# Four reorderings in a two-layer attention and MLP kernel: early split of the output weights, query features tile by tile, norm transposes behind output products, keys woven by fifths

## The chip, the cores and the metric

The kernel runs on one core of a Trainium2 chip. The metric is the time of one execution on the device in microseconds (us), the median of several runs. The engines are TensorE (PE, matrix products, with its weight loads counted apart as PEld), VectorE (DVE), ScalarE (ACT), GpSimd (POOL) and SyncE (SP), which issues nearly all of the DMA transfers. Each engine works through its own list of instructions in order and waits on semaphores for the others.

## The reference

Two equal layers follow each other on x of 2048 rows (S) by 576 columns (D), in f32. In each layer:

```
n = layernorm(x);  q, k, v = n @ wqkv                    # 32 heads of 18 columns
pq = q @ w_phi (per head);  pk = k @ w_phi
phi_q = [softmax(pq), softmax(-pq)];  phi_k likewise     # 36 features a head
kv = phi_k^T v;   z = sum of phi_k over the rows
x = x + ((phi_q kv) / (phi_q z + 1e-6)) @ wo
h = relu(layernorm(x) @ w1 + b1)^2                       # 4608 hidden columns
x = x + h @ w2 + b2
```

Keys of all rows are needed before the first query of a layer can be finished, since kv and z sum over all rows.

## The kernel before

**Tiles and precision.** The rows stand in four blocks of 512, each of four row tiles of 128. Every f32 operand of a large product is split in a high and a low part (names ending in h and l: ACT copies the high part, DVE or POOL subtracts it to leave the low one), and a product is three matrix products: high by high, low by high, high by low.

**Order of the work.** At the start the feature matrix w_phi is folded into the query and key weights (`g_fold`), which is woven with the norm of block 0. Then come the first keys: for three blocks `g_keys` projects v and k by row tile (v0, k0), makes the key features (K: DVE maxima, POOL and ACT for the exponentials, DVE sums, POOL scaling) and adds a tile to kv (kvp, two tiles later), woven with the next block's norm (n0). The last block's keys end in `barrier`, where z and the scaled kv matrices (ko, kt, kbh, kbl) are made, the queries' features of one block are finished (`g_phi`, names t0f in layer 0 and t1f in layer 1: products fm, sums fu, factors, scaled features fQ0e to fQ3e, one for each row tile), and `g_out` makes its attention output: transposes of the features (opt), products with kv (opn, split in ooh, ool and the last piece oolt), output products (opo) with the output weights (oo), added to x (ox). Its norm (onm, onn, one) and that norm's transposes (onp) follow in the same function. Then come the MLP of two blocks one by one (m with the block's number), and of the other two blocks as a pair (names m_p), whose second half is `seconds`: for each of 36 hidden tiles 12 products by rows (pach, pacacc0 to pacacc2) and 3 for the remaining features (pacacc3). In layer 0 that half is woven with `back_keys`, which norms a finished block for layer 1 (n1_3, n1_2, n1_0), projects its v and k and adds them to kv.

**The norm's transposes.** A norm makes four row tiles (n0 to n3). Each is transposed in four pieces on PE into a PSUM tile (p0 to p3), and the columns left over of two row tiles go into one further tile (p40, p41). ACT copies the high part out, DVE subtracts the low one (L413), and only then is the tile of PSUM free. The bank used by p40 is released by the subtraction for p0.

**What sets the order.** Generators are woven by hand: `weave(main, other, rate)` gives the second generator `rate` units of cost at every step of the first. A scheduler then places the instructions of each engine by priority in program order, and may take one ahead of another where its operands are ready by its own estimate. `tc.issue_after` keeps an instruction behind a given one; `held` does that for named instructions, and `chained` (L129) keeps everything that a step of a generator issues on DVE, ACT and POOL behind the last instruction that its earlier steps issued there, but leaves PE and SP free.

**Output weights.** In layer 0 `g_out` loads the raw output weights in the barrier (`wpiece`, L320 and L322), splits them there (ACT copies, and POOL subtracts, L331) and stores the parts in DRAM (wsoh, wsol, L352) for later loads; in layer 1 it loads the stored parts.

Of the kernel before, what the change touches and what calls it, by code (L numbers as in the profile page):

```python
# [21 lines left out]
def layers_kernel(  # L22
# [210 lines left out]
    def g_fold(kpair, vpair):  # L233
# [41 lines left out]
        def times(k, wt):  # L275
# [39 lines left out]
    def wpiece(src, c0, name, tags=TAGS_A, heads=False, low=None):  # L315
        raw = sb.tile([P, NC, HP], F32, tag="wraw", name=f"{name}r", bufs=2)
        hi, lo = piece_tiles(name, tags)
        if heads:
            full = (NG - 1) * GW
            nc.sync.dma_start(raw[:GW, : NG - 1],  # L320
                              src[:full, c0 : c0 + HP].rearrange("(g p) n -> p g n", p=GW))
            nc.sync.dma_start(raw[: gw[-1], NG - 1], src[full:, c0 : c0 + HP])  # L322
            parts = [(slice(0, GW), slice(0, NG - 1)), (slice(0, gw[-1]), slice(NG - 1, NG))]
        else:
            nc.sync.dma_start(raw[:, :KC],
                              src[: KC * P, c0 : c0 + HP].rearrange("(c p) n -> p c n", p=P))
            load_twice(raw[:, KC], src, c0, HP)
            parts = [(slice(0, P), slice(0, NC))]
        for p, c in parts:
            nc.scalar.activation(hi[p, c], raw[p, c], AF.Copy)  # L330
            (low or nc.vector).tensor_sub(lo[p, c], raw[p, c], hi[p, c].bitcast(F32))  # L331
        return hi, lo

    def wpair(which, name, tags=TAGS_A, low=None):
        if which in kept and tags is TAGS_A:
            return [wloaded(which, h, f"{name}{which}{h}", tags) for h in range(2)]
        if which == "o":
            return [wpiece(wo, h * HP, f"{name}o{h}", tags, heads=True, low=low) for h in range(2)]
        return [wpiece(wf, (which == "k") * D + h * HP, f"{name}{which}{h}", tags) for h in range(2)]

# [40 lines left out]
    def g_norm(x_of, dst, name, then=None, fine=False):  # L381
# [57 lines left out]

        if not fine:  # L440
# [302 lines left out]
    def g_out(layer, b, ph, dst, name, parts=1, pause=None, behind=None, norm=None, mid=None, costs=(None, None)):  # L743
# [46 lines left out]
        def pieces():  # L790
            with tc.issue_after(behind.ins) if behind else nullcontext():
                return wpair("o", name, low=nc.gpsimd if parts > 1 else None)

        def x_after(t):
# [3 lines left out]
            for half in range(2):  # L798
                hi, lo = pair[half]
                pt = wtile(f"{name}po{half}{t}")  # L800
                for g in range(NG):
                    w = gw[g]
                    l = ol[:w, g, rows] if g < KC else olt[:w, rows]
                    for k, (a, m) in enumerate(((oh[:w, g, rows], hi), (oh[:w, g, rows], lo), (l, hi))):
                        nc.tensor.matmul(pt[:, :HP], a, m[:w, g], start=(g == 0 and k == 0),  # L805
                                         stop=(g == NG - 1 and k == 2))
                cols = slice(half * HP, (half + 1) * HP)
                nc.vector.tensor_add(x[:, cols], pt[:, :HP], x[:, cols])
            return x

        pair = pieces() if behind or "o" in kept else None
        if pair:
            keep_split("o", pair)
# [11 lines left out]
        pair = pair or pieces()  # L825

# [4 lines left out]
        def x_next(t):  # L831
            return xs_of[t] if t < len(xs_of) else x_after(t)
# [12 lines left out]

    def g_mlp(layer, b, x, after, name, rest=None, then=None):
# [82 lines left out]
        if rest:  # L929
            with tc.issue_after(dense["hidden"].ins):  # L930
                drain(rest)
# [649 lines left out]
```

## Time and profile before

| | us |
|---|---|
| median of 3 runs | 2532.76 |
| lowest, highest | 2530.81, 2532.87 |
| the profiled execution | 2538.57 |
| its span in the profile | 2536.8 |
| PE busy in it | 2481.7 |
| DVE, ACT, POOL busy | 1570.9, 1265.5, 949.5 |

The profiled execution is 5.8 us above the median, and 1.8 us of it lie outside the span. The mean granted clock of PE is 0.992 of the full one. In the rows of the profile a name such as n_2p stands for all buffers of that name (p0 to p41 of the norm of block 2), "<-" separates what is written from what is read, and a bracket at the end tells how long the engine idled before the row and which instruction released it. L numbers are lines of the kernel before; the changed kernel's lines are some 7 to 24 higher.

### The profile page before, as it was taken

The page shows a single profiled execution, that of the slowest core. Times are in us where ns is not written, and L with a number is a line of the kernel's source. Part 1 is how long each engine was busy: PE and PEld are TensorE (multiplying, and loading weights), DVE is VectorE, ACT ScalarE, POOL GpSimd, SP SyncE. Part 2 cuts the span into 40 slices and gives each one's busy share as a digit, 9 for nine tenths or more (in the row PEclk, how much of TensorE's full clock was granted, in tenths as well). Part 3 has the DMA queues.
Part 4 walks back from the last instruction along what each step waited for, and adds up shares of the span by engine and source line. Part 5 has one row for each costly group of instructions (what it writes and reads, how often), then busy time and mean ns, then how long its engine had stood idle before and what let it go on. Part 6 is the DMA issues. An engine that isn't in the chain of part 4 may idle for free.

```text
span 2536.8 us, 41468 instructions
## 1 busy us (share of the span) xinstructions
PE 2481.7 (98%) x15108; PEld 2179.8 (86%) x15108; DVE 1570.9 (62%) x2514; ACT 1265.5 (50%) x2245; POOL 949.5 (37%) x1101
## 2 busy tenths in 40 slices
PE   8998999999999999999999989999999999999999
PEld 8997888889888888888889988888898888888888
DVE  6778848554856655554667679394548566555444
ACT  4344545443446666663333435454445466666642
POOL 3544312212325555551333333031123355565322
PEclk8999999999999999999999999999999999999999
DMA  9222643356434433328654134333563444333363
GB/s 326 79 69 91 196 116 85 103 164 213 133 119 125 143 114 99 113 93 295 206 180 148 47 128 150 102 99 98 166 222 112 129 130 142 116 96 109 112 199 127
DMA packets 249691, 348.52 MB, mean 137 GB/s; under 512 B 30158, under 2 KB 157262, under 8 KB 246926
## 3 DMA queue, kind: packets, MB, share of 16 engines
q1 hardware_dynamic: 248228, 343.18, 42.7%
q8 instruction: 118, 1.93, 0.3%
q10 hardware_dynamic: 1258, 2.70, 0.3%
q14 instruction: 87, 0.71, 0.1%
HBM read 279.46 MB, written 66.32 MB: 136 GB/s over the span
## 4 chain that ended last, share of the span: by engine, by line
PE 47%; DVE 3%; DMA 2%; ACT 1%; POOL 1%; issue 1%; SPq 0%; DVEq 0%; ACTq 0%; POOLq 0%
PE m_1ph L887 5%; PE m_0ph L887 4%; PE m_pacacc L1231 4%; PE m_ppx L1202 4%; PE m_1acc L914 3%; PE m_0acc L914 3%; PE m_pacc L1231 3%; PE m_ppy L1202 2%; PE m_pacacc L1221 2%; PE m_pach L1231 1%; PE m_0acc L905 1%; PE m_1acc L905 1%; PE m_pacc L1221 1%; PE m_ppz L1202 1%; PE a_0po L805 1%
## 5 line engine op out<-in xcount | busy, mean ns | idle before, releaser
L1192 POOL TENSOR_TENSOR m_ps<-m_pr,m_ps 128x128 fp32r<-128x128 f32 x144 | 118.2, 821 | 338.6 <-ACT m_ps L1190 282.9
L1191 DVE TENSOR_TENSOR m_ps<-m_pr,m_ps 128x448 fp32r<-128x448 f32 x144 | 98.1, 681 | 194.7 <-ACT m_ps L1190 191.3
L1231 PE MATMUL m_pacc<-m_ps,m_phb 128*128 128x448 f32 x864 | 188.5, 366 | 0.0
L1231 PEld LDWEIGHTS m_pacc<-m_ps,m_phb 128*128 128x128 f32 x864 | 162.2, 188 | 18.0
L1190 ACT ACTIVATE m_ps<-m_pr 128x576 fp32r<-128x576 f32 x144 | 98.1, 681 | 154.5 <-issue 88.2
L1231 PE MATMUL m_pacacc<-m_ps,m_phc 128*128 128x448 f32 x648 | 147.7, 370 | 0.0
L1231 PEld LDWEIGHTS m_pacacc<-m_ps,m_phc 128*128 128x128 f32 x648 | 122.6, 190 | 9.9
L1212 DVE TENSOR_TENSOR m_phb<-m_pz,m_phb 128x512 fp32r<-128x512 f32 x72 | 56.5, 784 | 113.1 <-ACT m_pz L1211 111.6
L914 PE MATMUL m_2acc<-m_2s,m_2hb 128*128 128x448 f32 x432 | 100.2, 366 | 0.0
L914 PE MATMUL m_0acc<-m_0s,m_0hb 128*128 128x448 f32 x432 | 100.1, 366 | 0.0
L887 PE MATMUL m_3ph<-t0onh,m_3h 128*128 128x512 f32 (+1 forms) x380 | 98.0, 383 | 1.6 <-DVE t0onh L426 0.8
L914 PE MATMUL m_1acc<-m_1s,m_1hb 128*128 128x448 f32 x432 | 99.4, 365 | 0.0
L914 PE MATMUL m_3acc<-m_3s,m_3hb 128*128 128x448 f32 x432 | 99.4, 365 | 0.0
L887 PE MATMUL m_1ph<-t1onh,m_1h 128*128 128x512 f32 (+1 forms) x380 | 97.8, 382 | 1.5 <-DVE t1onh L426 0.8
L887 PE MATMUL m_0ph<-a_0nh,m_0h 128*128 128x512 f32 (+1 forms) x380 | 97.8, 384 | 0.0
L887 PE MATMUL m_2ph<-a_2nh,m_2h 128*128 128x512 f32 (+1 forms) x380 | 97.8, 384 | 0.0
L914 PEld LDWEIGHTS m_2acc<-m_2s,m_2hb 128*128 128x128 f32 x432 | 80.9, 188 | 10.5 <-ACT m_2hb L895 0.2
L914 PEld LDWEIGHTS m_0acc<-m_0s,m_0hb 128*128 128x128 f32 x432 | 80.9, 188 | 10.6 <-ACT m_0hb L895 0.2
L914 PEld LDWEIGHTS m_1acc<-m_1s,m_1hb 128*128 128x128 f32 x432 | 81.1, 188 | 10.3
L914 PEld LDWEIGHTS m_3acc<-m_3s,m_3hb 128*128 128x128 f32 x432 | 81.1, 188 | 10.3
L872 POOL TENSOR_TENSOR m_3s<-m_3r,m_3s 128x128 fp32r<-128x128 f32 x36 | 24.6, 683 | 168.6 <-ACT m_3s L867 154.1
L872 POOL TENSOR_TENSOR m_1s<-m_1r,m_1s 128x128 fp32r<-128x128 f32 x36 | 24.7, 686 | 167.7 <-ACT m_1s L867 153.3
(2440 smaller groups left out, 7372.1 us busy)
## 6 DMA issues: line engine op xcount, KB each, us to landing
m_pr<-in_B_w SPq DMA_DIRECT2D x144, 288.0 KB
m_pr<-in_B_w SPq DMA_DIRECT2D x72, 256.0 KB
hd<-m_pu SPq DMA_DIRECT2D x72, 256.0 KB
m_pg<-hd SPq DMA_DIRECT2D x72, 256.0 KB
m_3r<-in_B_w SPq DMA_DIRECT2D x36, 288.0 KB
m_2r<-in_B_w SPq DMA_DIRECT2D x36, 288.0 KB
m_1r<-in_B_w SPq DMA_DIRECT2D x36, 288.0 KB
m_0r<-in_B_w SPq DMA_DIRECT2D x36, 288.0 KB
```

Source lines behind the costliest of these rows:

```text
L805: nc.tensor.matmul(pt[:, :HP], a, m[:w, g], start=(g == 0 and k == 0), stop=(g == NG - 1 and k == 2))
L872: nc.gpsimd.tensor_sub(s2[:, D + R : 2 * D], r2[:, R:], s2[:, R:D].bitcast(F32))
L887: dense["hidden"] = nc.tensor.matmul(ph[:, cols], a, m, start=(k == 0), stop=(k == len(ops) - 1))
L905: nc.tensor.matmul(acc[KC], a, m, start=(f == 0 and k == 0), stop=(f == NF - 1 and k == 2))
L914: nc.tensor.matmul(acc[t][:, :R], a[:, rows], m, start=(f == 0 and k == 0), stop=(f == NF - 1 and k == 2))
L1190: nc.scalar.activation(s2[:, :D], r2, AF.Copy)
L1191: nc.vector.tensor_sub(s2[:, D : D + R], r2[:, :R], s2[:, :R].bitcast(F32))
L1192: nc.gpsimd.tensor_sub(s2[:, D + R : 2 * D], r2[:, R:], s2[:, R:D].bitcast(F32))
L1202: nc.tensor.matmul(ps, a, m, start=start and i == 0, stop=i == len(ms) - 1, skip_group_check=True)
L1212: nc.vector.tensor_sub(hl, r, hh.bitcast(F32))
L1221: nc.tensor.matmul(accs[b][KC], a, m, start=(g == 0 and k == 0), stop=(g == NF - 1 and k == 2))
L1231: nc.tensor.matmul(accs[b][t][:, :R], a[:, rows], m, start=(g == 0 and k == 0), stop=(g == NF - 1 and k == 2))
```

## The change

**V's split in the fold.** In `g_fold` the split of the v weights runs one chunk behind.

**Output weights.** A new generator `g_split` loads the raw output weights in five groups (wsr0 to wsr4, four of 126 rows and one of 72), splits each (wss: high part on ACT, low part on DVE) and stores both parts in DRAM. `g_keys` advances it by one step at each row tile of the first keys. The barrier of layer 0 now loads the split parts as layer 1 does; the loads, copies, POOL subtractions and stores that it had are gone. The raw groups use the buffers named r2, which the first hidden tiles' weights use too, and the split groups use the two places of kbh and kbl.

**Query features.** In `barrier` the generator `g_phi` is wrapped in `chained`.

**Norm in the barrier.** `g_out` with two parts no longer draws the norm step by step between the output products: it scales two row tiles, makes the output products, and issues the transposes of a row tile behind a named last output product. The last tile's part is a function that the MLP calls.

**Keys' side.** `seconds` yields five times for a hidden tile (after the products of each row tile and after the remaining features) in place of once, the rate of the weave goes from 4.0 to 0.8, and `chained` gets a strict form that also keeps PE's instructions of `back_keys` behind those that stand ahead of them in the program.

```diff
-    def chained(gen):
+    def chained(gen, strict=False):
...
             mark = len(traced)
+            if strict:
+                ends[nc.tensor.engine] = next(i for i in reversed(traced) if i.engine == nc.tensor.engine)
             with ExitStack() as behind:
...
+            for c in ([c - 1] if i == 2 and c else []) + ([c] if i == 2 and c == KC else []):
                 for half in range(2):
                     hi, lo = (piece[:, c] for piece in vpair[half])
...
+    def g_split():
+
+        for g in range(NG):
+            w = gw[g]
+            raw = sb.tile([P, D], F32, tag="r2", name=f"wsr{g}")
+            nc.sync.dma_start(raw[:w], wo[g * GW : g * GW + w])
+            both = cst.tile([P, 2 * NG * GW], F32R, tag=("kbh", "kbl")[g % 2], name=f"wss{g}")
+            hi, lo = both[:w, :D], both[:w, D : 2 * D]
+            nc.scalar.activation(hi, raw[:w], AF.Copy)
+            yield
+            nc.vector.tensor_sub(lo, raw[:w], hi.bitcast(F32))
+            for part, home in zip((hi, lo), wsplit["o"]):
+                nc.sync.dma_start(home[:w].rearrange("p (h c n) -> p h c n", h=2, c=NC)[:, :, g],
+                                  part.rearrange("p (h n) -> p h n", h=2).bitcast(F32))
+            yield
...
-        pair = pieces() if behind or "o" in kept else None
-        if pair:
-            keep_split("o", pair)
+        pair = wpair("o", name)
...
-        norms = (norm or g_norm)(x_next, dst, f"{name}n", keep)
-        for t in range(len(xs_of)):
-            for _ in held(norms, ("part",)):
-                break
-        if xs_of:
-            for _ in range(NT - len(xs_of)):
-                next(norms)
-            dense["rest"] = norms
+        if not xs_of:
+            yield from paced((norm or g_norm)(x_after, dst, f"{name}n", keep), costs[1])
             return
-        yield from paced(norms, costs[1])
+        scale, turn_rows, turn_rest = next(g_norm(xs_of.__getitem__, dst, f"{name}n", keep, None))
+
+        def behind_out(call, *args):
+            with tc.issue_after(dense["out"].ins):
+                call(*args)
+
+        with tc.issue_after(dense["part"].ins):
+            xns = [scale(t) for t in range(2)]
+        xs_of.append(x_after(2))
+        behind_out(turn_rows, 0, xns[0])
+        other = g_after(3)
+        next(other)
+        behind_out(turn_rows, 1, xns[1])
+        behind_out(turn_rest, 0)
+        xs_of.append(next(other))
+        xns.append(scale(2))
+        behind_out(turn_rows, 2, xns[2])
+        xns.append(scale(3))
...
-                second(f)
+                for t in range(NT):
+                    by_rows(f, [t], range(3))
+                    yield
+                features(f, range(3))
+                del high[f], wide[f]
                 yield
...
-        phi = g_phi(layer, er, ph, f"{n}f")
+        phi = chained(g_phi(layer, er, ph, f"{n}f"))
...
+    splits = g_split()
...
             yield
+            next(splits, None)
             e = soft_k(raw, f"K0_{b}_{t}")
...
-        back = iter(()) if layer else chained(back_keys())
+        back = iter(()) if layer else chained(back_keys(), True)
...
-        weave(seconds, back, 4.0)
+        weave(seconds, back, 0.8)
```

The first place is SP's list in the first keys, before and after (x0_2 is the input of block 2, xth and xtl are spills of a norm, t0q0r raw query weights):

```order
L467 DMA xtl0_105<-n0_0l_385 128x2048
L1357 DMA x0_2_0_1148<-in_A_x 128x576
L1357 DMA x0_2_1_1226<-in_A_x 128x576
L1357 DMA x0_2_2_1356<-in_A_x 128x576
L1357 DMA x0_2_3_1424<-in_A_x 128x576
L325 DMA t0q0r_2333<-wf_109 128x4x288
L227 DMA t0q0r_2333<-wf_109 64x288 x2
L325 DMA t0q1r_2341<-wf_109 128x4x288
```

```order
L337 DMA wsr2_1118<-in_A_wo 126x576
L1381 DMA x0_2_0_1166<-in_A_x 128x576
L1381 DMA x0_2_1_1244<-in_A_x 128x576
L1381 DMA x0_2_2_1377<-in_A_x 128x576
L344 DMA wsoh_116<-wss2_1120 252x1x288
L337 DMA wsr3_1402<-in_A_wo 126x576
L1381 DMA x0_2_3_1449<-in_A_x 128x576
L1381 DMA x0_3_0_1707<-in_A_x 128x576
L321 DMA t0q0r_2368<-wf_109 128x4x288
L344 DMA wsol_117<-wss2_1120 252x1x288
L344 DMA wsoh_116<-wss3_1404 252x1x288
L337 DMA wsr4_1659<-in_A_wo 72x576
```

The load of wsr3 and the last of x0_2 now stand behind a store of wss2, and the load of wsr4 behind a store of wss3; both stores wait for subtractions on DVE.

The second place is POOL's list in the barrier of layer 0, before and after (oo0l and oo1l are low parts of the output weights, fm the products and fQe the scaled features of the queries):

```order
L331 TENSOR_TENSOR t0oo0l_2992<-t0oo0r_2990,t0oo0h_2991 126x1152
L331 TENSOR_TENSOR t0oo0l_2992<-t0oo0r_2990,t0oo0h_2991 72x288
L331 TENSOR_TENSOR t0oo1l_3001<-t0oo1r_2999,t0oo1h_3000 126x1152
L694 TENSOR_TENSOR t0fm01_2836<-t0fQ0e_2549,zb0_2802 128x576
L331 TENSOR_TENSOR t0oo1l_3001<-t0oo1r_2999,t0oo1h_3000 72x288
L694 TENSOR_TENSOR t0fm11_2913<-t0fQ1e_2556,zb0_2802 128x576
L712 TENSOR_TENSOR t0fQ0e_2549<-t0fQ0e_2549,t0fQ0r_2626 128x576
L694 TENSOR_TENSOR t0fm21_2981<-t0fQ2e_2630,zb0_2802 128x576
L712 TENSOR_TENSOR t0fQ1e_2556<-t0fQ1e_2556,t0fQ1r_2700 128x576
```

```order
L704 TENSOR_TENSOR t0fm01_2871<-t0fQ0e_2584,zb0_2837 128x576
L722 TENSOR_TENSOR t0fQ0e_2584<-t0fQ0e_2584,t0fQ0r_2661 128x576
L704 TENSOR_TENSOR t0fm11_2948<-t0fQ1e_2591,zb0_2837 128x576
L722 TENSOR_TENSOR t0fQ1e_2591<-t0fQ1e_2591,t0fQ1r_2735 128x576
L892 TENSOR_TENSOR m0_3s2_0_3503<-m0_3r2_0_3497,m0_3s2_0_3503 128x128
L704 TENSOR_TENSOR t0fm21_3016<-t0fQ2e_2665,zb0_2837 128x576
```

The four subtractions of the output weights are gone, and the product for the second row tile (fm11) stands behind the scaling of the first (fQ0e).

The third place is PE's list where the norm of block 2 for layer 1 meets the hidden tiles 48 and 49 of the pair, before and after:

```order
L1231 MATMUL m0_pacacc1_11997<-m0_ps2_48_12687,m0_phc48_12693 128x448 x3
L1231 MATMUL m0_pacacc2_11998<-m0_ps2_48_12687,m0_phc48_12693 128x448 x3
L1221 MATMUL m0_pacacc3_11999<-m0_phc48_12693,m0_ps2_48_12687 128x512 x3
L404 MATMUL n1_2p0_12911<-ident_157,n1_2n0_12817 128x128 x4
L404 MATMUL n1_2p1_12920<-ident_157,n1_2n1_12830 128x128 x4
L1231 MATMUL m0_pach_11995<-m0_ps2_49_12750,m0_phc49_12756 128x448 x3
L1231 MATMUL m0_pacacc0_11996<-m0_ps2_49_12750,m0_phc49_12756 128x448 x3
L418 MATMUL n1_2p40_12927<-ident_157,n1_2e_12806 128x128 x2
L1231 MATMUL m0_pacacc1_11997<-m0_ps2_49_12750,m0_phc49_12756 128x448 x3
L1231 MATMUL m0_pacacc2_11998<-m0_ps2_49_12750,m0_phc49_12756 128x448 x3
L1221 MATMUL m0_pacacc3_11999<-m0_phc49_12756,m0_ps2_49_12750 128x512 x3
L404 MATMUL n1_2p2_12958<-ident_157,n1_2n2_12869 128x128 x4
```

```order
L1251 MATMUL m0_pacacc1_12018<-m0_ps2_48_12708,m0_phc48_12714 128x448 x3
L411 MATMUL n1_2p0_12926<-ident_157,n1_2n0_12829 128x128 x4
L1251 MATMUL m0_pacacc2_12019<-m0_ps2_48_12708,m0_phc48_12714 128x448 x3
L411 MATMUL n1_2p1_12938<-ident_157,n1_2n1_12851 128x128 x4
L1241 MATMUL m0_pacacc3_12020<-m0_phc48_12714,m0_ps2_48_12708 128x512 x3
L425 MATMUL n1_2p40_12948<-ident_157,n1_2e_12818 128x128 x2
L1251 MATMUL m0_pach_12016<-m0_ps2_49_12771,m0_phc49_12777 128x448 x3
L411 MATMUL n1_2p2_12967<-ident_157,n1_2n2_12881 128x128 x4
L1251 MATMUL m0_pacacc0_12017<-m0_ps2_49_12771,m0_phc49_12777 128x448 x3
L1251 MATMUL m0_pacacc1_12018<-m0_ps2_49_12771,m0_phc49_12777 128x448 x3
L411 MATMUL n1_2p3_12977<-ident_157,n1_2n3_12903 128x128 x4
L1251 MATMUL m0_pacacc2_12019<-m0_ps2_49_12771,m0_phc49_12777 128x448 x3
```

The transposes now stand between the products of single row tiles, and those of the remainder (n1_2p40) stand ahead of the six products pach and pacacc0 of hidden tile 49, behind which they stood.

More of the change, by code (lines that the diff above doesn't have):

```diff
@@ L741, in g_features, with g_out @@
                                  (2.6, 0.4, 3.0, 2.8, 1.2)), ("last", "squared"))
-    def g_out(layer, b, ph, dst, name, parts=1, pause=None, behind=None, norm=None, mid=None, costs=(None, None)):
+    def g_out(layer, b, ph, dst, name, parts=1, pause=None, norm=None, mid=None, costs=(None, None)):
         kbh, kbl = sums[layer]["kb"]
@@ L788, in times, with g_after @@
                 dense["part"] = nc.vector.tensor_sub(lo, pn[:w, :pw], oh[:w, g, cols].bitcast(F32))
[L790 to L794, printed above, removed]
+        def g_after(t):
             x = sb.tile([P, D], F32, tag="x", name=f"{name}x{t}", bufs=5)
@@ L1371, in g_attend @@
             yield from mid[0]
-        yield from g_out(layer, b, ph, dst, name, behind=behind and behind["last"], norm=norm, mid=mid[1],
+        yield from g_out(layer, b, ph, dst, name, norm=norm, mid=mid[1],
                          costs=(1.0, None if norm else 3.0))
```

48 lines of the change are left out of this document (21 added, 27 removed).

## Prediction

> **What bounds the kernel now.** I read the page's busy times first, then the table of waits for TensorE (PE), then a table of stages with the granted clock, and last single stretches of the engines in order of time.
>
> ```profile
> PE 2481.7 (98%) x15108; PEld 2179.8 (86%) x15108; DVE 1570.9 (62%) x2514; ACT 1265.5 (50%) x2245; POOL 949.5 (37%) x1101
> ```
> ```profile
> PE n_2p L418 <- DVE n_2l L413: 6.1, 1, 6.1
> PE n_0p L418 <- DVE n_0l L413: 5.6, 1, 5.6
> PE t0opt L768 <- DVE t0fQ1e L712: 3.5, 1, 3.5
> ...
> PE t1onp L404 <- DVE t1onn L393: 2.3, 3, 1.3
> PE t0onp L404 <- DVE t0onn L393: 2.3, 3, 1.3
> PE kt L631 <- DVE kq L625: 2.2, 1, 2.2
> PE t1opt L768 <- DVE t1fQ1e L712: 2.0, 1, 2.0
> PE k_3kp L484 <- DMA w_3k0h<-wskh: 1.9, 1, 1.9
> PE n_3p L418 <- DVE n_3l L413: 1.8, 1, 1.8
> ...
> PE t0opt L768 <- DVE t0fQ0e L712: 1.2, 1, 1.2
> ```
> ```profile
> 30.00:180.00 150.00, 148.12 (x1800) 144.92 (x1801) 112.76 (x181) 57.54 (x114) 66.60 (x58) 0.98 0.41 145
> 180.00:260.00 80.00, 68.60 (x742) 65.58 (x742) 67.41 (x122) 30.68 (x67) 40.33 (x33) 0.96 0.29 96
> ...
> 1180.00:1386.00 206.00, 192.43 (x1595) 177.21 (x1594) 127.56 (x177) 72.91 (x125) 71.90 (x69) 0.96 0.57 195
> ...
> 1470.00:1520.00 50.00, 43.25 (x322) 41.03 (x322) 38.24 (x88) 18.74 (x47) 20.29 (x21) 0.97 0.40 138
> ```
> PE is busy 98% of the time, and the number of matrix products stays the same, so only two things can move: its idle time (2536.8 − 2481.7 = 55 us of span) and a lowered clock. In the table of stages the columns are PE, PEld, DVE, ACT, POOL, then PE's granted clock. The idle time lies where the change works: the barrier of layer 0 (180 to 260: 11.4 us), the keys woven behind the last hidden tiles (1180 to 1386: 13.6 us) and the barrier of layer 1 (1470 to 1520: 6.8 us). These stretches also have the low clocks: 0.96 over 206 us is up to 8.2 us of speed, less what of it falls on idle time. One such place, groups of the same product before and after the 6.1 us wait:
>
> ```profile
> 1238.91 1.96 PE L1231 MATMUL m_pacacc<-m_ps,m_phc 128*128 128x448 f32 x9
> ...
> 1252.91 0.69 PE L418 MATMUL n_2p<-ident,n_2e 128*128 128x128 f32 x2 [6.13 <-DVE n_2l L413]
> 1253.25 2.59 PE L1231 MATMUL m_pacacc<-m_ps,m_phc 128*128 128x448 f32 x6
> ```
> One product takes 1.96 / 9 = 0.22 us before and 2.59 / 6 = 0.43 us after: a wait costs its length and then some 2 us of halved clock. In layer 1 a wait of only 2.0 us is followed by the same (0.97 over 50 us is 1.5 us).
>
> **Output weights split early.** In the barrier of layer 0, POOL subtracts four pieces of the output weights; layer 1, which loads split weights, has no such work and is the model of after. Product z begins both stretches, the last low part (oolt) ends them:
>
> ```profile
> 195.96 2.01 PE L589 MATMUL z<-kv,top 128*128 128x126 f32 x16
> ...
> 228.00 0.42 DVE L788 TENSOR_TENSOR t0oolt<-t0opn,t0ooh 72x256 fp32r<-72x256 f32 x1 [0.82 <-ACT t0ooh L786]
> ```
> ```profile
> 1456.64 1.99 PE L589 MATMUL z<-kv,top 128*128 128x126 f32 x16
> ...
> 1482.97 0.42 DVE L788 TENSOR_TENSOR t1oolt<-t1opn,t1ooh 72x256 fp32r<-72x256 f32 x1 [0.83 <-ACT t1ooh L786]
> ```
> 32.0 us against 26.3 us: **−5.7 us**. The cause shows on VectorE (DVE) and POOL:
>
> ```profile
> 198.04 3.94 POOL L331 TENSOR_TENSOR t0oo0l<-t0oo0r,t0oo0h 126x1152 fp32r<-126x1152 f32 x2 [4.82 <-ACT t0oo0h L330]
> ...
> 201.38 7.77 DVE L605 TENSOR_TENSOR kbl<-ko,kbh 126x504 fp32r<-126x504 f32 x2
> ...
> 1462.01 2.37 DVE L605 TENSOR_TENSOR kbl<-ko,kbh 126x504 fp32r<-126x504 f32 x2
> ```
> The same two subtractions take 7.77 us beside POOL's and 2.37 us without, 5.4 us of the 5.7. [...]
>
> The new place is the first keys: five loads, five ACT copies, five DVE subtractions and ten stores, all in a stage where PE is busy 148.12 of 150 us. What covers them is the slack of the keys:
>
> ```profile
> 68.64 0.41 ACT L502 ACTIVATE k_0s<-k_0p 128x288 f32<-128x288 f32 x1 [0.62 <-PE k_0p L484]
> ...
> 74.69 1.17 ACT L528 ACTIVATE K_3e<-K_3e 128x1152 f32<-128x1152 f32 x1 [2.05 <-DVE n_1h L426]
> ```
> ```profile
> 78.30 2.15 POOL L544 TENSOR_TENSOR K_3e<-K_3e,K_3r 128x1152 f32<-128x1152 f32 x1 [3.64 <-DVE K_3r L533]
> ...
> 88.79 2.15 POOL L544 TENSOR_TENSOR K_0e<-K_0e,K_0r 128x1152 f32<-128x1152 f32 x1 [3.55 <-ACT n_2h L412]
> ```
> ```profile
> 87.98 0.77 PE L573 MATMUL kvp<-K_3e,vslot 128*32 128x36 f32 x64
> ...
> 96.93 0.77 PE L573 MATMUL kvp<-K_0e,vslot 128*32 128x36 f32 x64
> ```
> ```profile
> DMA  8999920576747009999896910000000000810000
> ```
> ```profile
> 47.34 11.52 SPq L1357 DMA_DIRECT2D x<-in_A_x  x4
> ```
> ```profile
> 61.31 0.75 DVE L375 BATCH_NORM_STATS2 n_2s<-x 128x6 f32<-128x288 f32 x2
> ```
> PE uses K_3 at 87.98, ready at 80.45, and the next K_0 at 96.93, ready at 90.94: 7.5 and 6.0 us of slack. SP works in order. There wsr3 is now loaded behind the store of wss2, which waits for DVE at about 72, and so is the last x of block 2. How long a landing takes lies between some 1.1 us (288 KB at 274 GB/s, the rate before 30 us) and 14.0 us (the x issued at 47.34, used at 61.31, with the DMA full). The DMA's busy tenths above run from 60 us in slices of 1 us: from 65 on it has gaps and stands at 0 at 73 and 74, so I estimate 2.5 to 3: wsr3 lands at 75.3, while ACT stands before its copy from 68 on, with k_0s behind it. K_3 then comes 5 us late (cover left: 2.5). wsr4 in turn stands behind the store of wss3 (about 86) and lands at 89; ACT waits for it with the evictions behind it. PE has seven tiles of PSUM to run ahead, 1.9 us each; the eighth is wanted at 88.7 and free at 89.7, and K_0 is 1 us late as well: **+2 us** (0 with the quick landing, +18 with the slow one). The V split that lags a chunk, on ACT before 40 us, I cost at nothing, since the same copies and subtractions are issued, some a chunk later; bounds ±1 by estimate.
>
> **Query features by tile.** On DVE the product fm20 and its sum no longer stand ahead of fQ1e, for which PE waits:
>
> ```profile
> 1470.59 1.73 DVE L694 TENSOR_TENSOR t1fm<-t1fQ2e,zb 128x576 f32<-128x576 f32 x1
> ...
> 1472.38 0.74 DVE L700 TENSOR_REDUCE t1fu<-t1fm 128x32 f32<-128x576 f32 x1
> 1473.04 1.34 DVE L712 TENSOR_TENSOR t1fQ1e<-t1fQ1e,t1fQ1r 128x576 f32<-128x576 f32 x1
> ```
> ```profile
> 1461.29 1.95 POOL L694 TENSOR_TENSOR t1fm<-t1fQ1e,zb 128x576 f32<-128x576 f32 x1
> ```
> That takes 2.47 us out; but POOL's fm11, done at 1463.2 before, now stands behind POOL's half of fQ0e, and DVE must wait for it. Counting the chain through, fQ1e comes 1.6 us earlier. I take **−1.5 us in each layer, −3.0**, near the wait it shortens. Ends: +0.8 (the serial fm11 is the longer chain) and −3.7 (the wait of 2.0 and its 1.5 to 1.7 us of clock go whole).
>
> **Norm's transposes behind output products.** In each layer three waits of 2.3 us together (onp). The transposes move behind 5 to 12 more output products, about to the point where the rows are scaled. **−2.0 in each layer, −4.0.** Ends: 0 (the DVE chain of the norm is the bound and the wait returns at the next hidden product) and −4.6.
>
> **Keys' side by fifths.** Three norms stall PE by 1.8 + 6.1 + 5.6 us. PE wants the remainder's transposes (p40), whose PSUM bank comes free with DVE's n_l, late in this chain:
>
> ```profile
> 1249.40 0.67 DVE L393 TENSOR_SCALAR n_2n<-x,n_2m,n_2d 128x512 f32<-128x512 f32 x1 [0.98 <-POOL n_2d L378]
> ...
> 1252.16 1.29 DVE L413 TENSOR_TENSOR n_2l<-n_2p,n_2h 128x512 fp32r<-128x512 f32 x2
> ```
> After the change p40 stands 8, 6 and 9 to 12 products of 0.22 us earlier on PE in the three norms: 1.8, 1.3 and 2.0 to 2.6 us more to wait. DVE's chain comes earlier too, since the projections ahead do: 0.6, about 2 and 0 to 2 us. So n_3p 3.0, n_2p 5.4, n_0p 6 or so: 14.4 against 13.5. **+1.0 us**, nothing taken for the next key weights (k_2kp), whose load gets less time before its use; it may come to wait as k_3kp's does, 1.9 us. Ends: −15.7 (the waits of n_2p and n_0p go, with 4 us of clock) and +11.
>
> [...]
>
> **The sum.** The profiled execution took 2538.57 us, 1.8 us of it outside the span, and lies 5.8 us above the median of 2532.76. −5.7 + 2 − 3 − 4 + 1 = −9.7 us: 2528.9 by the profiled execution, **2523** by the median.
>
> **Rivals.**
> - The fifths do feed PE: DVE catches up behind smaller pieces, and the two long waits go with their clock. For it speaks that PE's supply is finer; against it that p40 stands earlier. −15.7 in place of +1: 2506.
> - The first keys stall (slower): wsr3 lands after 14 us as the x did, at 86.6. ACT's evictions stop, PE runs out of PSUM tiles near 82 (5 us), K_3 misses its slack by 4, wsr4 costs 3, and two halved stretches 6: +18 in place of +2, 2539. Against it: the DMA is no longer full at 72. It decides from a landing past 84 or so.
> - The stalls of the fifths grow to the upper end, +11 in place of +1 (n_0p 2.6, n_3p and its clock 2.9, n_2p 2, key weights 1.9 with 1.6 of clock): 2533, no change.
> - The two reorderings in the barriers don't do what they say, as the norm's and the features' chains on DVE are as long as before: 0 in place of −7, 2530.
>
> **Chances.** Forecast 0.48 (its own range 2517 to 2530), fifths feed 0.10, first keys stall 0.15, fifths' stalls grow 0.15, reorderings empty 0.12. About 0.2%, 5 us, is what a measurement of this kernel can tell from no change: 2527.7 to 2537.8. Faster: 0.43 + 0.10 + 0.03 = 0.56; slower: 0.11 from the first keys and 0.04 from the fifths = 0.15; the rest, 0.29, is the same. The range leaves out most of the fifths' gain and the worst of the first keys: 2512 to 2540.
>
> **What would show it.** Right: kbl<-ko,kbh near 2.4 us in both layers; the waits for kq and t0fQ0e gone, for fQ1e under 1 us; no onp wait over 0.5 us; n_2p and n_0p still waiting 4 us or more; no PE wait over 2 us between 60 and 110. Wrong: evictions on ACT behind wss3 or wss4 with PE idle there; or the n_p waits gone, or longer than 7 us.

## The result, and the profile after

| | before | after |
|---|---|---|
| median of the runs shown | 2532.52 us (4 runs) | 2553.24 us (4 runs, 2551.80 to 2554.89) |
| ratio to before, 95% interval | 1 | 1.0083 [1.0066, 1.0101] |
| profiled execution | 2538.57 us, span 2536.8, clock 0.992 | 2554.89 us, span 2553.2, clock 0.990 |

The change makes the kernel 20.7 us slower. The forecast was 2523 us, and its range ended at 2540.

The page of the changed kernel, busy times; as many products as before, 7.8 us more of them (part of them at half clock), and 8.6 us more idle time of PE (2553.2 − 2489.5 against 2536.8 − 2481.7):

```profile
PE 2489.5 (98%) x15108; PEld 2186.2 (86%) x15108; DVE 1567.1 (61%) x2519; ACT 1265.0 (50%) x2246; POOL 944.3 (37%) x1097
```

The table of PE's waits of the changed kernel (who was waited for, us in total, times, longest):

```profile
PE n_0p L425 <- DVE n_0l L420: 4.7, 1, 4.7
PE n_2p L425 <- DVE n_2l L420: 4.6, 1, 4.6
...
PE kvp L583 <- issue: 3.6, 1, 3.6
PE t0opt L778 <- DVE kbl L615: 3.0, 1, 3.0
PE t1opt L778 <- DVE kbl L615: 3.0, 1, 3.0
PE t1opt L778 <- DVE t1fQ3e L722: 2.9, 1, 2.9
PE t0opt L778 <- DVE t0fQ3e L722: 2.9, 1, 2.9
...
PE a_3qp L494 <- issue: 2.1, 1, 2.1
...
PE n_3p L425 <- DVE n_3l L420: 1.5, 2, 1.1
PE t1onp L411 <- DVE t1onn L400: 1.4, 3, 0.7
PE t0onp L411 <- DVE t0onn L400: 1.3, 2, 0.7
```

The waits that the change aimed at are shorter: fQ1e is gone from the top, the onp waits fell from 2.3 us a layer to 1.4 and 1.3, the three norms of the woven keys wait 10.8 us in place of 13.5. Six others stand in their place: kbl and fQ3e in both layers (11.8 us, against 0.9 for each fQ3e before, shown below), and two waits for "issue", in the kvp products of layer 0 and at the first product of a_3q in layer 1. Before the change:

```profile
PE t1opt L768 <- DVE t1fQ3e L712: 0.9, 1, 0.9
```

The changed kernel's table of the stages that the prediction showed (stretch, PE, PEld, DVE, ACT, POOL, PE's granted clock, DMA share, GB/s):

```profile
30.00:180.00 150.00, 146.85 (x1788) 143.30 (x1788) 118.53 (x181) 56.19 (x115) 67.36 (x57) 0.98 0.46 159
180.00:260.00 80.00, 67.93 (x712) 65.31 (x711) 59.27 (x115) 27.64 (x64) 30.83 (x25) 0.91 0.22 69
1180.00:1386.00 206.00, 195.88 (x1625) 180.35 (x1626) 125.05 (x181) 76.25 (x132) 71.81 (x71) 0.98 0.60 206
1470.00:1520.00 50.00, 41.72 (x288) 39.72 (x287) 36.49 (x81) 16.66 (x43) 20.82 (x19) 0.90 0.20 62
```

The loss lies in the two barriers. Their clock fell from 0.96 to 0.91 and from 0.97 to 0.90, and in the first of them PE passes 712 products in the 80 us shown where it passed 742 (its work there starts 1.1 us later). The woven keys (third row) are better than before, with clock 0.98 against 0.96.

Matching PE's products of the two profiles by name gives the offset of after to before from place to place: +2.2 us in the first keys, +7.0 in the barrier of layer 0, −6.4 in the woven keys, +11.4 in the barrier of layer 1, and +2.2 in the rest, together the 16.4 us by which the span grew.

**Where VectorE stops.** DVE of the changed kernel in the barrier of layer 1, from fQ1e to the two last low parts of the attention output (oolt):

```profile
1476.14 0.76 DVE L722 TENSOR_TENSOR t1fQ1e<-t1fQ1e,t1fQ1r 128x576 f32<-128x576 f32 x1
1476.82 1.72 DVE L704 TENSOR_TENSOR t1fm<-t1fQ2e,zb 128x576 f32<-128x576 f32 x1
1480.24 1.41 DVE L710 TENSOR_REDUCE t1fu<-t1fm 128x32 f32<-128x576 f32 x2 [1.70 <-POOL t1fm L704]
1481.57 0.29 DVE L615 TENSOR_TENSOR kbl<-kt,kbh 72x144 fp32r<-72x144 f32 x1
...
1490.56 0.42 DVE L798 TENSOR_TENSOR t1oolt<-t1opn,t1ooh 72x256 fp32r<-72x256 f32 x1 [0.82 <-ACT t1ooh L796]
...
1508.98 0.42 DVE L798 TENSOR_TENSOR t1oolt<-t1opn,t1ooh 72x256 fp32r<-72x256 f32 x1 [0.59 <-ACT t1ooh L796]
```

The same stretch of POOL:

```profile
1476.25 1.67 POOL L722 TENSOR_TENSOR t1fQ1e<-t1fQ1e,t1fQ1r 128x576 f32<-128x576 f32 x1 [2.72 <-DVE t1fQ1r L717]
1477.89 0.97 POOL L892 TENSOR_TENSOR m_1s<-m_1r,m_1s 128x128 fp32r<-128x128 f32 x1
1478.82 1.39 POOL L704 TENSOR_TENSOR t1fm<-t1fQ2e,zb 128x576 f32<-128x576 f32 x1
```

And PE, which waits for the subtraction kbl<-kt and then runs at half clock (granted clock 0.50 from 1480.9 to 1487.7 us; 0.42 us for one product of this form, 0.27 ahead of the wait):

```profile
1478.69 0.27 PE L778 MATMUL t1opt<-ident,t1fQ1e 128*126 128x128 f32 x1
1481.92 0.48 PE L778 MATMUL t1opt<-ident,t1fQ0e 128*126 128x128 f32 x1 [2.96 <-DVE kbl L615]
...
1482.40 0.42 PE L778 MATMUL t1opt<-ident,t1fQ1e 128*126 128x128 f32 x1
```

The chained order took fm20, fm21 and their sums away from ahead of fQ1e, and put them between fQ1e and the next things that PE wants: kbl and the pieces t1of. DVE also stands still for 1.70 us there, because fm21 on POOL now stands behind POOL's own half of fQ1e (and behind 0.97 us of hidden weights, m_1s, that came between). Nor did fQ1e itself come 1.6 us earlier: counted from the start of z in layer 1, DVE's half ended at 17.3 us in place of 17.7, and POOL's at 18.3 in place of 17.1.

**Where TensorE's instructions come late.** The group of kvp products of tile K3, before and after, then the place in PE's order of time in the changed kernel:

```profile
L573 PE MATMUL kvp<-k_3K3e,vslot x64: 193/197/221, 194.0 to 195.2; 128*32 128x36 f32 x64
```

```profile
L583 PE MATMUL kvp<-k_3K3e,vslot x64: 193/197/221, 195.1 to 199.5; 128*32 128x36 f32 x64
```

```profile
195.08 0.64 PE L583 MATMUL kvp<-k_3K3e,vslot 128*32 128x36 f32 x48
199.37 0.34 PE L583 MATMUL kvp<-k_3K3e,vslot 128*32 128x36 f32 x16 [3.65 <-issue]
```

The DMA from 186 to 206 us, in slices of 0.5 us (busy tenths), first before the change, then of the changed kernel, with the queues of the whole stretch (packets, MB, share):

```profile
DMA  0010000000000100000010000498861988799889
```

```profile
DMA  0000010095589897898899988730010000000000
...
q1 hardware_dynamic: 896, 2.65, 39.6%
q8 instruction: 3, 0.05, 1.1%
```

From 190 to 199.5 us the DMA engines are busy 0.84 of the time (0.09 before the change) with the eight loads of split output weights, at 280 GB/s. In the same stretch PE gets its instructions, in packets of 16 KB on queue q8 (118 of them, 1.93 MB, in the execution). (That they are PE's is worked out: from one packet to the next PE starts 256 of its 30216 products and weight loads in the median, in both profiles, and this count spreads by 0.2 of its mean, that of every other engine by 0.5 to 0.8.) The records of the single packets put them at 196.7 and 200.5 us, where they stood at 192.8 and 196.2 before the change. PE runs dry after 48 of 64 products; that it waits for instructions there is so far inferred, and experiment 5 tests it.

### The profile page after: what moved, and what is told of

Its sections match the earlier page's. It is cut to its first block, busy times and chain, and to the rows that moved or that the text cites. A ratio compares the mean times of both kernels' runs of the same rounds, so it can differ in the third digit from the quotient of the medians.

```text
span 2553.2 us, 41484 instructions
## 1 busy us (share of the span) xinstructions
PE 2489.5 (98%) x15108; PEld 2186.2 (86%) x15108; DVE 1567.1 (61%) x2519; ACT 1265.0 (50%) x2246; POOL 944.3 (37%) x1097
## 3 DMA queue, kind: packets, MB, share of 16 engines
q8 instruction: 118, 1.93, 0.3%
## 4 chain that ended last, share of the span: by engine, by line
PE 84%; DVE 6%; POOL 3%; ACT 2%; DMA 2%; issue 2%; SPq 1%; DVEq 0%; POOLq 0%; ACTq 0%
PE m_ppx L1222 8%; PE m_pacc L1251 6%; PE m_3ph L907 5%; PE m_1ph L907 4%; PE m_0ph L907 4%; PE m_2ph L907 4%; PE m_pacacc L1251 4%; PE m_ppy L1222 4%; PE m_3acc L934 3%; PE m_1acc L934 3%; PE m_0acc L934 3%; PE m_2acc L934 3%; PE m_ppz L1222 2%; PE m_pacc L1241 2%; PE m_pacacc L1241 2%
```

## The experiments

**1. Plain features.** The chained form is undone; all else of the change stays, and PE's own order is the same.

```diff
-        phi = chained(g_phi(layer, er, ph, f"{n}f"))
+        phi = g_phi(layer, er, ph, f"{n}f")
```

> The changed kernel, but the query features are again one plain generator: fm20, fm21 and their sums stand on VectorE ahead of fQ1e, as before the change; everything else of the change stays, and TensorE's own order is the same. Theory (order on VectorE): what the chained form took from ahead of fQ1e it put between fQ1e and the two things that TensorE wants next, kbl and the t?of pieces. The waits for kbl (2.96 us in each layer) and for fQ3e (2.9) go back to under 1 us each, fQ1e waits come back (about 3.5 and 2.0), and with the halved clock behind them the time falls by 8 to 14 us against the changed kernel, to about 2540 to 2545. Rival (the features' order is harmless and the waits move only with the rest of the barrier): within 3 us of the changed kernel, 2550 to 2556. Second rival (my forecast of the chained form was right by itself): 3 us slower than the changed kernel, 2556.

Measured: 2534.68 us (10 runs), ratio to before 1.0006 [0.9997, 1.0016]. That is 18.6 us below the changed kernel, more than the theory's 14. PE's waits in the barrier of layer 1, of this kernel:

```profile
PE t1opt L778 <- DVE t1fQ1e L722: 2.3, 1, 2.3
PE t1opt L778 <- DVE t1fQ3e L722: 0.9, 1, 0.9
```

How long the two halves of the barrier take can be read from product z and the two last low parts (oolt). For this kernel, z in layer 1, then oolt:

```profile
L599 PE MATMUL z<-kv,top x16: 275/275/314, 1451.2 to 1452.9; 128*128 128x126 f32 x16
```

```profile
1476.33 0.42 DVE L798 TENSOR_TENSOR t1oolt<-t1opn,t1ooh 72x256 fp32r<-72x256 f32 x1 [0.82 <-ACT t1ooh L796]
...
1491.21 0.42 DVE L798 TENSOR_TENSOR t1oolt<-t1opn,t1ooh 72x256 fp32r<-72x256 f32 x1 [0.59 <-ACT t1ooh L796]
```

For the changed kernel, z in layer 1:

```profile
L599 PE MATMUL z<-kv,top x16: 274/275/309, 1459.6 to 1461.3; 128*128 128x126 f32 x16
```

| us | before | after | plain features |
|---|---|---|---|
| z to the first oolt, layer 0 | 32.0 | 31.4 | 26.4 |
| z to the first oolt, layer 1 | 26.3 | 31.0 | 25.1 |
| first to second oolt, layer 0 | 14.9 | 18.2 | 14.9 |
| first to second oolt, layer 1 | 14.9 | 18.4 | 14.9 |

The four differences between the last two columns add up to 17.7 us, nearly the whole 18.6. Up to half of it is clock. The mean span over the listed executions, times one less the mean granted clock, is what the lowered clock can cost at most: 26.2 us after (4 executions, 2551.6 us), 17.0 with plain features (10, 2532.4), 16.4 before (32, 2530.4). So of 19.2 us of mean span the chained form costs up to 9.2 in clock, and the other 10.0 in waits and order.

**2. and 3. The two halves of the chained form.** One kernel chains the first five steps only (the last of them makes fm20, fm21 and their sums), the other only the three from the sixth on (fm30, fm31). The expectations count one step too few; the instructions that they name are those of the edits.

```diff
-        phi = chained(g_phi(layer, er, ph, f"{n}f"))
+        phis = g_phi(layer, er, ph, f"{n}f")
+        phi = chained(phis)
...
-        drain(g_out(layer, b, ph, dst, f"{n}o", 2, phi))
+        drain(g_out(layer, b, ph, dst, f"{n}o", 2, phis))
```

> The changed kernel with the features chained in their first four steps only (fm20, fm21 and their sums behind fQ1e); from the fifth step on VectorE's order is again that of before. The wait for kbl (2.96 us in each layer) should stay and the wait for fQ3e fall from 2.9 to 0.9. Theory (the two places add up, each its wait with the halved clock behind it): 7 to 11 us below the changed kernel, 2542 to 2546. Rival (the first place alone makes the 18.6 us, since the barrier then only shifts): 2551 to 2554.

```diff
-        phi = chained(g_phi(layer, er, ph, f"{n}f"))
+        phi = g_phi(layer, er, ph, f"{n}f")
...
-        drain(g_out(layer, b, ph, dst, f"{n}o", 2, phi))
+        drain(g_out(layer, b, ph, dst, f"{n}o", 2, chained(phi)))
```

> The other half: the first four steps as before the change, chained from the fifth on (fm30, fm31 and their sums behind fQ2e). The waits for kbl should go, those for fQ1e come back (about 2.3 and 1.9), the wait for fQ3e stay at 2.9. Theory (the places add up): 8 to 12 us below the changed kernel, 2541 to 2545, and this half's gain and the other half's make 18.6 us together, within 4. Rival (only one of the two counts): one of the two kernels stands at 2534 to 2537 and the other at 2551 to 2554.

Measured: 2544.90 us with the first half chained (5 runs), within the 2542 to 2546 expected, and 2538.28 with the second (7 runs), below the 2541 to 2545 expected: 10.2 and 3.6 us above the plain features. The waits are where they were expected. With the first half chained, kbl waits 3.0 us in each layer and fQ3e 0.9; with the second, kbl is gone, fQ1e waits 1.9 and 1.8 us and fQ3e 2.9. Together the halves make 13.8 us of 18.6; reckoned from the runs of before beside each (2533.21 us there, 2532.11 here) it is 11.3 and 4.7, 16.0 of 19.2. So 4.8 us are missing by the medians, outside the theory's margin of 4, and 3.2 by the runs of before, inside it: that the places add up holds roughly at best, and the rival, one half for all, not at all. The missing part seems to be clock: without it (mean span less the share above) the halves stand 8.6 and 3.3 us above the plain features and both together 10.0, while the clock's share grows by 0.3, 2.6 and 9.2.

**4. The chained form alone,** on the kernel before.

```diff
-        phi = g_phi(layer, er, ph, f"{n}f")
+        phi = chained(g_phi(layer, er, ph, f"{n}f"))
```

> The kernel before with the chained features alone, nothing else of the change. Theory (the chained order is bad by itself): 15 to 20 us slower than before, 2548 to 2553, with waits for kbl and fQ3e near 3 us in layer 1. Rival (it is bad only beside the early split or the moved transposes): under 6 us slower, below 2539. My forecast's term was 3 us faster, 2530.

Measured: 2544.01 us (4 runs), 1.0057 [1.0039, 1.0074], 11.9 us slower: bad by itself, but between the theory's 15 and the rival's 6. PE's waits in this kernel:

```profile
PE t0opt L768 <- DVE t0fQ1e L712: 5.6, 1, 5.6
...
PE t1opt L768 <- DVE kbl L605: 3.0, 1, 3.0
PE t0opt L768 <- DVE t0fQ3e L712: 2.9, 1, 2.9
PE t1opt L768 <- DVE t1fQ3e L712: 2.9, 1, 2.9
```

Layer 1 waits as in the changed kernel. In layer 0 fQ1e already waited 3.5 us before, and z to oolt grows only from 32.0 to 34.3 us, against 26.4 to 31.4 where the output weights are split early. So some of the 18.6 us is, by these profiles, a gain of the early split that the chained form keeps from showing.

**5. Loads held back.** The eight loads of split output weights in layer 0's barrier are meant to wait for four one-element writes into their tiles, which stand behind the first feature product on POOL. The four large ones (567 KB each) are issued at 204.5 to 205.8 us in place of 189.3 to 192.0; three of the small ones (81 KB) still are at 192.5 to 194.4.

```diff
+        if behind is not None:
+            with tc.issue_after(behind.ins):
+                for piece in pair:
+                    nc.gpsimd.memset(piece[:1, 0, :1].bitcast(F32), 0.0)
...
-        pair = wpair("o", name)
+        pair = ([wloaded("o", h, f"{name}o{h}", TAGS_A, dense["fm"]) for h in range(2)]
+                if parts > 1 and layer == 0 else wpair("o", name))
```

> The changed kernel, with the eight loads of split output weights in the barrier of layer 0 held back to about 204 us by four one-element writes into their tiles behind the first feature product on GpSimd; nothing else. Theory (the loads fill the DMA engines from 189 to 199 us and TensorE's instructions, 16 KB at a time, come 4 us late behind them): the stop in the middle of the 64 kvp products (3.6 us, put down to issue) falls under 0.6 us, the two fetches land near 193 and 197 as before the change, and the time is 4 to 7 us below the changed kernel, about 2547 to 2549. Rival (the stop has another cause): the wait stays near 3.6 us and the time within 2 us of the changed kernel, or above it where the output products now wait for weights.

Measured: 2546.24 us (4 runs), 7.0 us below the changed kernel. The group of kvp products and the DMA of this kernel in the same stretch:

```profile
L587 PE MATMUL kvp<-k_3K3e,vslot x64: 192/197/222, 198.3 to 199.0; 128*32 128x36 f32 x64
```

```profile
DMA  0000000000100004322301000001000000000029
```

The 64 products take 0.7 us from the first start to the last, in place of 4.4, with nothing put down to issue. The packets of instructions lie at 196.6 and 200.0 us, the first of them 1.1 us behind the start of the kvp products of K2; in the changed kernel it was 4.3 us, and 1.6 before. What held PE was the load burst: the theory holds.

**6. Plain features and loads held back,** both edits together.

> The changed kernel with the plain features and with the held-back loads of output weights. Theory (the two causes are independent): the 18.6 us of the first and the 7.0 us of the second add up, 2526 to 2530, 3 to 7 us faster than before, no stop over 0.6 us within the kvp products. Rival (the 7 us of the held-back loads were halved clock that the plain order has removed already): 2532 to 2535, no faster than the plain order alone.

Measured: 2529.07 us (10 runs), 0.9990 [0.9979, 1.0000]. The held-back loads gain 5.6 us here (4.5 reckoned from the runs of before beside each), 7.0 beside the chained form: the two causes add up within that. This kernel is 3.0 us below before in the same runs, about 0.1%, at the edge of what is told from no change.

**7. and 8. The norm's transposes in their old order,** in the changed kernel and in the kernel of experiment 6.

```diff
-        with tc.issue_after(dense["part"].ins):
-            xns = [scale(t) for t in range(2)]
-        xs_of.append(x_after(2))
-        behind_out(turn_rows, 0, xns[0])
...
+        norms = (norm or g_norm)(x_next, dst, f"{name}n", keep)
+        for t in range(len(xs_of)):
+            for _ in held(norms, ("part",)):
+                break
```

> The changed kernel with the norm behind the output products in its old order (transposes as the norm yields them, the loads of the next unit in their old order), everything else as changed. Theory (the moved transposes gain about 1 us a layer, but the changed order of loads behind the barrier makes TensorE wait 2.1 us for a_3q's first product in layer 1, with 3.4 us of halved clock): the onp waits are 2.3 us together in each layer again, the wait of a_3qp goes, and the time is 0 to 3 us below the changed kernel. Rival (the transposes gain the 2.0 us a layer that I forecast and a_3qp's wait has nothing to do with it): 4 us slower than the changed kernel, a_3qp still waiting about 2 us.

> The plain features and held-back loads (2529.1 us), now with the norm behind the output products in its old order. Theory (the moved transposes gain the 1 us a layer that the onp waits show, and the 7.2 us that undoing them gained in the changed kernel were the a_3qp wait and halved clock, which the plain order has removed): 1 to 3 us slower, 2530 to 2532. Rival (the moved transposes cost 7 us wherever they stand): 2520 to 2523.

Measured: 2546.01 us in the changed kernel (4 runs, 2541.28 to 2551.21), 7.2 us below it, and 2529.01 us in the other (11 runs), where it makes 0.1 us of difference. With the old order the waits of onp are 2.3 us a layer again; PE of the second kernel:

```profile
PE t1onp L415 <- DVE t1onn L404: 2.3, 3, 1.3
PE t0onp L415 <- DVE t0onn L404: 2.3, 3, 1.3
```

So the moved transposes do shorten those waits by about 1 us a layer, and the time doesn't show it: for the second kernel I expected 1 to 3 us, the rival 7 us the other way, and neither came. In the changed kernel the 7.2 us are more than the 3 at most that I expected; up to 5.2 of them are clock (21.0 us of lost clock in place of 26.2, reckoned as in experiment 1). Its profile with the old order gains 3.7 us at the end of layer 1's barrier, where a_3qp's wait of 2.1 us and a halved stretch at 1532 are gone.

That wait, put down to issue, is one for a load. The product reads a_3uh (1280 KB, 128 packets of 10 KB). In all nine profiled kernels with the norm's new order it waits, by 0.2 to 2.1 us, and starts 0.4 us behind the end of the last of these packets (after: 1531.3 and 1531.7). In all five with the old order it doesn't wait, and the last packet ends 0.5 to 1.7 us ahead of it. SP's list shows what differs, before and after:

```profile
1511.10 0.37 SPq L471 DMA_DIRECT2D a_3uh<-xth  x1
...
1522.44 0.59 SPq L352 DMA_DIRECT2D a_3q0l<-wsql  x1
```

```profile
1517.94 0.44 SPq L359 DMA_DIRECT2D a_3q0l<-wsql  x1
...
1522.31 0.37 SPq L481 DMA_DIRECT2D a_3uh<-xth  x1
```

With the norm's new order the 720 KB of a_3q0l go ahead of a_3uh, and from its issue to its last packet a_3uh takes 7.1 to 9.0 us, in place of 6.0 (7.2 in one kernel). So the theory on the loads holds as far as the wait goes: the edit brings it, though no run changes the loads' order without the transposes. What makes its length vary (0.7 us in experiment 6, so that little was left to gain there) isn't settled.

**9. to 11. The fifths of the keys' side:** undone in the changed kernel and in the kernel of experiment 6, and alone on the kernel before.

```diff
-                for t in range(NT):
-                    by_rows(f, [t], range(3))
-                    yield
-                features(f, range(3))
-                del high[f], wide[f]
+                second(f)
                 yield
...
-        back = iter(()) if layer else chained(back_keys(), True)
+        back = iter(()) if layer else chained(back_keys())
...
-        weave(seconds, back, 0.8)
+        weave(seconds, back, 4.0)
```

> The changed kernel with the keys' side of the second chunk woven whole again (one step for a feature group, the old rate, no link to TensorE), everything else as changed. Theory (the fifths gain, as the offset between the two traces over 1160 to 1400 us says, 6.4 us): 5 to 8 us slower than the changed kernel, 2558 to 2561, with n_2p and n_0p waiting 6.1 and 5.6 us again and the wait for the key weights of k_3kp back. Rival (the forecast: the fifths cost 1 us, and the 6.4 us are the clock's luck in one execution): 0 to 2 us faster than the changed kernel, 2551 to 2553.

> The plain features and held-back loads of the run before (2529.1 us), now with the keys' side of the second chunk woven whole again. Theory (the fifths gain what the profiles show, 4 to 6 us over 1160 to 1400 us, and the changed kernel's barriers hid it in halved clock): 4 to 6 us slower, 2533 to 2535. Rival (they gain nothing, as undoing them in the changed kernel moved its median by 0.0): 2527 to 2531.

> The kernel before with the fifths of the keys' side alone. Theory (the fifths gain 4 to 6 us): 2526 to 2528, n_2p and n_0p waiting 4.6 and 4.7 us in place of 6.1 and 5.6, no wait for the key weights of k_3kp. Rival (nothing gained, as in the changed kernel): 2531 to 2534. My forecast's term was 1 us slower.

Measured: 2553.28 us (4 runs, 0.0 to the changed kernel), 2529.69 (11 runs, 0.6 above experiment 6) and 2532.26 (11 runs, 1.0001 [0.9992, 1.0010] to before). PE's waits from 1160 to 1400 us of the kernel with the fifths alone:

```profile
PE n_0p L420 <- DVE n_0l L415: 4.7, 1, 4.7
PE n_2p L420 <- DVE n_2l L415: 4.6, 1, 4.6
PE n_3p L420 <- DVE n_3l L415: 1.5, 2, 1.1
```

The waits are 10.8 us where they were 15.4 before (with the 1.9 of k_3kp), and yet there is no gain of 4 to 6 us. My theory falls in all three, and the rivals hold. The profiles misled me: they are single executions, and that of before lay 5.8 us above its median while that of the fifths alone lay 3.2 below its own. From 1160 to 1400 us the offset to before falls by 4.0 and 2.8 us even in the two kernels with the fifths undone, against 6.4 and 5.5 in the same kernels with them: before's profile was slow there. Where the 4.6 us of shorter waits go isn't settled; a gain of up to 2 us is within the interval, and so is a loss of as much.

**12. Loads of the split issued ahead.** In the kernel of experiment 6, each load of output weights among the first keys is issued ahead of the stores of the group before it.

```diff
             nc.vector.tensor_sub(lo, raw[:w], hi.bitcast(F32))
+            if g + 1 < NG:
+                load(g + 1)
             for part, home in zip((hi, lo), wsplit["o"]):
```

> The plain features and held-back loads (2529.1 us), and in the split among the first keys each load of output weights is issued ahead of the two stores of the group before it, where it stood behind them. Theory (ScalarE and VectorE reach K_0 and K_1 late because the loads of wsr3 and wsr4 stand behind stores that wait for VectorE): the wait of k_1p's first product for ScalarE (2.2 us, with clock behind it) goes and the time is 2 to 4 us lower, 2525 to 2527. Rival (VectorE is late by the subtractions themselves): within 1 us, the wait still near 2.

Measured: 2529.43 us (11 runs), 0.4 above experiment 6. ACT copies the last piece at 73.8 us in place of 80.8 in experiment 6, and PE still waits:

```profile
PE k_1p L505 <- ACT vslot L514: 2.0, 1, 2.0
```

The rival holds: the loads are not what makes the first keys late.

## Why the prediction was wrong

- **Query features by tile: the step that failed.** I wrote that fm20 and its sum "no longer stand ahead of fQ1e, for which PE waits", and took −1.5 us in each layer with +0.8 as the worst. That they leave that place is true, and fQ1e's long wait went. What I left out is what they stand ahead of instead: kbl and the pieces t?of, and further on fQ3e. I counted the chain as far as fQ1e and stopped at the wait that was being removed, and even so far it was wrong: fQ1e came 0.4 us earlier on DVE and 1.2 later on POOL in layer 1, where I had 1.6 earlier. Measured: +18.6 us with the rest of the change, +11.9 alone, in place of −3.0. By the forecast's other steps alone the time would have stood near the one before (2534.68).
- **Output weights split early: the mechanism right, a cost missed.** In the changed kernel kbl fell to two pieces of 0.67 and 0.69 us in layer 0, and with plain features z to oolt takes 26.4 us there where 26.3 was forecast from layer 1. But the loads moved too: the raw weights were loaded at 170 to 176 us into buffers of their own, and the split parts, twice as many bytes, are loaded at 189 to 193. I gave that no price. They delayed PE's instructions: 4.5 to 7.0 us, as much as the gain.
- **The first keys: the size about right, the reason wrong.** The offset of the profiles there is +2.2 us after (+1.7 to +4.5 in the other kernels with the split), against +2. I put it down to loads behind stores on SP; with the loads ahead it stayed at +4.5. That points to the chain of the features on DVE and POOL, which now holds the five subtractions; this part is argued only. No run has the early split alone, and none undoes the lag of V's split, which I cost at nothing.
- **Norm's transposes: half the size, and nothing of it in the time.** −2.0 a layer was forecast for the waits; they shortened by 0.9 and 1.0, and with plain features and held-back loads the medians differ by 0.1 us. The edit also moved the load of a_3uh behind another, which I gave no price: 0.7 us of wait there, and 2.1 in the changed kernel, where undoing the edit gained 7.2 us.
- **The fifths: 0 ± 2 measured, +1.0 forecast,** for a reason that was wrong in detail. I had n_2p at 5.4 and n_0p at 6 us after the change; they are 4.6 and 4.7, so in these profiles DVE's chain came earlier by more than p40 did.
- **The rivals.** None of the four was it. The last had the barriers, but with waits that stay as long as before; that a reordering could lengthen a barrier by more than the wait that it removes was in none, and so the range ended too low. The third counted 1.7 us of clock for n_3p, half of a stretch of 3.4 us such as before's records have behind the wait of 2.0 us for t1fQ1e (from 1475.8 us); after, n_3p waited 1.5 us and no stretch at half clock began between 262.4 and 1255.6 us. The signs named for being right had the same blind spot: kbl<-ko,kbh did shorten, the waits for kq and t0fQ0e went, and n_2p and n_0p still waited over 4 us, while the time rose, for most of the signs watched the waits that the change aimed at.

The steps as measured, each kernel against the runs of before beside it: −3.0 us for the change with plain features and held-back loads, +1.5 with the loads in their place (4.5 more), +20.7 with the chained features as well (19.2 more). In another order the steps come out otherwise, as experiments 4 and 7 show.

## What to carry to other kernels

When an instruction is moved out of the way of a wait, follow it to its new place and ask who waits for what stands behind it there; a chain that puts two engines' steps strictly one after the other can also expose the slower engine's time, as where DVE stood still for 1.70 us behind POOL's fm21. When work is replaced by loads, price the moment at which they start, and all that shares the DMA engines then, here TensorE's own instructions too (3.65 us); a wait put down to issue was here one for a load (2.1 us) and one for instructions (3.65), so look at what lands as it ends. And a saving read from two single profiles is worth less than its size while stretches at half clock, 1.7 us of loss or more each (half of 3.4), come and go from one execution to the next (mean granted clock of the kernel before: 0.992 to 0.995): ask the median.

## What the runs showed of the hardware

- **Instructions queue behind data.** With the DMA engines busy 0.84 of 9.5 us, 16 KB of PE's instructions came some 3 us late (4.3 us behind the start of K2's kvp products, in place of 1.6), and PE stood for 3.65 us in the middle of a group of small products (64 in 0.7 us). Nothing in the table of waits names the DMA: the wait is put down to issue, as is the one of 2.1 us for the load of a_3uh.
- **The halved clock comes in a grid.** In the profiles before and after, the records of the granted clock hold 1 and 0.5 and nothing between. The starts of the 8 and 12 stretches at 0.5 lie whole multiples of 3.413 us apart in each, within 2 ns, and they last 3.41 or 6.83 us, but for the last of each, at the very end (1.5 and 2.5 us). After, in layer 1's barrier, they start at 1480.9, 1501.4 and 1532.1 us, 6 and 9 steps apart. Waits shorter than one step had such stretches by them: one of 3.4 us began 0.4 us behind the wait of 2.1 us for a_3qp, and one of 6.8 us began 1.9 us into the wait of 2.96 us for kbl.
- **Lost clock doesn't add up.** The two halves of the chained form alone added 0.3 and 2.6 us of lost clock (at most, as in experiment 1), both together 9.2, from 4 to 10 executions each; the means are uncertain by some 1 to 2 us. A reason for that was not tested.
